# Reordering the opening of a linear-attention and MLP kernel: tile 0 alone, new load order, tile 2's x ahead of tile 3's chain

## Chip, cores, metric

The kernel runs on one core of a Trainium2 chip. The metric is the device time of one execution in microseconds (us). Most figures in the text come from profiles: a profile is the record of one execution, and its span, from the first instruction to the last, is about 2 us shorter than the time. Engines are written as in the profile: PE is TensorE, PEld its weight loads, DVE is VectorE, ACT is ScalarE, POOL is GpSimd, SP is SyncE.

## The reference

Eight batches, eight heads, 576 positions, head size 64. The attention has no softmax:

```python
kv  = einsum('bhsd,bhse->bhde', k, v)
out = einsum('bhsd,bhde->bhse', q, kv)
out = out / sqrt(mean(out*out, -1) + 1e-6) * g_norm            # per head
x   = out, heads side by side                                  # (8, 576, 512)
xn  = (x - mean(x)) / sqrt(var(x) + 1e-6) * g_ln
y   = x + relu(xn @ w1) @ w2                                   # 512 -> 2048 -> 512
```

Inputs and output are float32; the products run in bfloat16.

## The kernel before

Work is done in tiles of 128 positions; batch 0 has four (t[0] to t[3]), and 64 positions remain (`J` in the code). For each tile the chain is:

- PE turns (transposes) q, ACT copies it out of PSUM;
- PE multiplies by kv (`o`), ACT squares (`sq`), DVE sums per head (`red`), ACT takes the root (`root`), DVE inverts it (`inv`);
- DVE scales (`y`, `x`, or `x_g` in one step from a product with kv already times g), and makes the centred, bfloat16 `xc`;
- PE turns `xc`, ACT copies it out as `xT`.

Then comes the first MLP product (`mm1`): 16 groups for the four tiles of batch 0, each of 16 matmuls and followed by a relu on ACT. The second product (`mm2`) follows.

Later batches are prepared while PE is busy with the products of earlier ones. An agenda does this: `at(slot, fn)` emits `fn` just before group number `slot` of the products. Only batch 0 has no earlier products to hide behind, so its opening is written by hand:

```python
    fill(18)                       # unread matmuls on zeros, while the loads are under way
    kv_first()                     # kv of batch 0: two head pairs, copies, two more pairs, copies
    ...                            # (cut: helpers)
    half_turn(0)                   # tiles 0 and 1 together, in halves of heads
    fill(2, ps_out, "ops")
    half_o(0, 0)
    half_turn(1)
    half_o(1, 0)
    half_o(0, 1)
    half_red(0, 0)
    half_red(0, 1)
    half_o(1, 1)
    t[0].root()
    half_red(1, 0)
    half_red(1, 1)
    t[0].o_g(ps1, "p1")
    t[1].o_g(ps1, "p1")
    fill(8)
    t[0].x_g()
    t[1].root()
    halves_turn(0, halves_xc(0), ps_out, "ops")
    t[1].x_g()
    xc1 = list(halves_xc(1))
    ...                            # (cut)
    at(1, lambda: turn_first(2, ps_m, "misc", nc.vector.tensor_copy))
    at(1.1, lambda: halves_turn(1, xc1, ps_out, "ops"))
    at(1.2, o2)                    # t[2]: o, sq
    at(1.3, x2)                    # t[2]: red, y, x, xc
    at(4, lambda: turn_first(3, ps_m, "misc"))
    at(5, lambda: t[3].o())
    at(5.1, x3)                    # t[3]: sq, red, y, x, xc   (y asks for the root)
    at(6, lambda: t[2].turn(True)) # xc of tile 2: turn and copy
    at(9, lambda: turn_first(J, ps_m, "misc"))
    at(9.5, next_loads)
    at(10, lambda: t[3].turn(True))
    ...                            # (cut)
    for ts, c0, c1 in ((0, 0, 8), (1, 0, 8), (0, 8, 12), (1, 8, 12), (0, 12, 16), (1, 12, 16),
                       (2, 0, 16), (3, 0, 16)):
        mm1(0, ts, 1, c0, c1)      # tile ts, column blocks c0 to c1; a group is 4 blocks
```

The loads of batch 0 are issued in this order: k (two queues), then on one queue v in two halves, q of tiles 0 and 1 in two halves of heads, the first quarter of w1, the rest of q, the rest of w1, half of w2, batch 1, the rest of w2.

## Time and profile before

| | before |
|---|---|
| time, median of 3 runs | 291.57 us (291.55 to 291.79) |
| span of the profiled run | 289.6 us |
| PE busy | 281.9 us (97%) |
| first kv matmul | 7.56 us |
| tile 0's x turned (first transpose of `xc`) | 15.04 us |
| first product without a break from | 18.25 us |
| second product of batch 0 from | 33.37 us |
| first product of batch 1 from | 50.39 us |

The page of the kernel before, cut to three of its lines. Part 1 gives each engine's busy us, share of the span and number of instructions. In part 2 each character is a fortieth of the span (7.2 us) and gives the busy share in tenths; PEclk is the clock granted to TensorE, in tenths of full speed.

```profile
PE 281.9 (97%) x2312; PEld 158.6 (55%) x2312; DVE 151.0 (52%) x335; ACT 155.0 (54%) x339; POOL 41.0 (14%) x68
...
PEclk9999999999999999999999999999999999999999
DMA  7999999469999918995997179938202510131033
```

PE is the limit (97%), and the transfer engines are nearly full up to 50 us (0.7 in the first slice, 0.9 or more in the six after it). The timeline of the kernel before shows where PE is not full. Columns: start in us, length in us, engine, source line, operation, output<-inputs, number of instructions merged; in brackets the idle time before, and what ended it.

```profile
7.56 0.19 PE L219 MATMUL even<-v_in,k_in 64*64 64x64 bf16 x1 [0.72 <-DMA v_in<-in_v_dram]
...
15.04 0.68 PE L541 MATMUL tp<-identity,xc 128*128 128x128 bf16 x4 [0.84 <-DVE xc L532]
...
18.25 2.84 PE L402 MATMUL p<-xT_blk,w_sb 128*128 128x128 bf16 x48
...
26.63 0.75 DVE L321 SCALAR_TENSOR_TENSOR xc<-x_blk,st_blk,g_ln_sb 128x512 bf16<-128x512 f32 x1
...
27.79 0.39 PE L337 MATMUL tp<-identity,xc 128*128 128x128 bf16 x4
28.01 5.52 PE L402 MATMUL p<-xT_blk,w_sb 128*128 128x128 bf16 x96
33.37 4.48 PE L418 MATMUL p<-w_sb,m 128*128 128x512 bf16 x20
```

From 28.01 us PE does not stop: 96 matmuls in 5.52 us, then the second product. Whatever the opening saves, the rest of the kernel can only be shifted by. Tile 3's `xc` ends at 27.38 us (26.63 + 0.75), just before PE turns it at 27.79.

The chain of waits of the kernel before, from 22 to 26 us (start, length, what the end of the program is followed back to):

```profile
22.51 0.24 ACT m L405
...
23.00 0.60 ACT sq L266
...
23.62 0.70 DVE ss L287
...
24.34 0.30 ACT rms L297
24.64 0.48 ACT m L405
25.13 0.48 ACT xT_blk L339
```

This is the place that one part of the change is after. ACT squares tile 3 (23.00), then stands until DVE has summed, takes the root (24.34), then does a relu, and only then copies tile 2's `xT` (25.13), for which PE waits; the next entry of the chain is PE at 25.66.

### The profile page before, as it was taken

Reading aid. Unit: us, or ns where it says so; the run is one execution under the profiler, and the core shown is the slowest. Engines: PE = TensorE matmul, PEld = TensorE weight load, DVE = VectorE, ACT = ScalarE, POOL = GpSimd, SP = SyncE. Lnnn points to the kernel's source line nnn. Section 1 sums busy time; section 2 is a strip of 40 time slices with the busy share of each in tenths; the row PEclk is TensorE's granted clock in tenths of the full one; section 3 lists DMA queues with packets and bytes.
Section 4 is the critical chain, followed back from the end, with each engine's and each line's share of the span. In section 5 each row is a group of like instructions: output and inputs, shape, how many; then the busy total and the mean of one; then the engine's idle time right before and its main releaser. Section 6 shows DMA issues by size and latency. Waiting matters only on the chain.

```text
span 289.6 us, 5791 instructions
## 1 busy us (share of the span) xinstructions
PE 281.9 (97%) x2312; PEld 158.6 (55%) x2312; DVE 151.0 (52%) x335; ACT 155.0 (54%) x339; POOL 41.0 (14%) x68
## 2 busy tenths in 40 slices
PE   7889999999999999999999999999999999999995
PEld 2579755996569644444444444444444444444444
DVE  5775028847997793765366925762578300220022
ACT  3467755885469832882189418920894076016500
POOL 8522520032032003200410023000000000000000
PEclk9999999999999999999999999999999999999999
DMA  7999999469999918995997179938202510131033
GB/s 215 203 206 203 201 202 218 109 99 188 155 177 160 151 40 158 205 167 102 148 208 103 42 146 194 178 75 164 54 18 53 112 36 0 38 81 28 0 74 73
DMA packets 64378, 36.10 MB, mean 125 GB/s; under 512 B 31836, under 2 KB 59356, under 8 KB 64352
## 3 DMA queue, kind: packets, MB, share of 16 engines
q0 software_dynamic: 28016, 17.76, 44.2%
q1 hardware_dynamic: 35824, 17.25, 30.5%
q10 hardware_dynamic: 512, 0.72, 0.7%
q8 instruction: 18, 0.29, 0.4%
q14 instruction: 8, 0.07, 0.1%
HBM read 36.71 MB, written 9.44 MB: 159 GB/s over the span
## 4 chain that ended last, share of the span: by engine, by line
PE 93%; DMA 2%; ACT 1%; DVE 1%; POOL 1%; issue 1%; POOLq 0%
PE p L418 43%; PE p L402 43%; PE o_ps L260 3%; DMA q_in<-in_q_dram 2%; PE kv_ps L235 2%; PE tp L183 1%; PE p L196 1%; PE tp L337 1%; ACT sq L266 0%; PE tp L170 0%; PE o_half L500 0%; POOL v_in L126 0%; ACT xT_blk L542 0%; ACT m L405 0%; DVE x_blk L278 0%
## 5 line engine op out<-in xcount | busy, mean ns | idle before, releaser
L402 PE MATMUL p<-xT_blk,w_sb 128*128 128x128 bf16 (+2 forms) x1024 | 131.8, 286 | 0.2
L418 PE MATMUL p<-w_sb,m 128*128 128x512 bf16 (+2 forms) x608 | 129.2, 368 | 0.0
L405 ACT ACTIVATE m<-p 128x512 bf16<-128x512 f32 x144 | 85.5, 596 | 43.3 <-PE p L402 41.1
L402 PEld LDWEIGHTS <-w_sb 128*128 128x128 bf16 x1024 | 78.5, 98 | 44.1 <-issue 0.6
L418 PEld LDWEIGHTS <-m 128*128 128x128 bf16 x608 | 56.8, 98 | 61.8
L423 DVE SCALAR_TENSOR_TENSOR o_sb<-p,rstd,x_blk 128x512 f32<-128x512 f32 (+2 forms) x38 | 27.4, 721 | 54.3 <-PE p L418 48.7
L266 ACT ACTIVATE sq<-o_ps 128x512 f32<-128x512 f32 x34 | 20.2, 595 | 41.5 <-PE o_ps L260 41.4
L287 DVE TENSOR_REDUCE ss<-sq 128x8 f32<-128x512 f32 x34 | 23.0, 678 | 11.2 <-ACT sq L266 11.2
L329 ACT ACTIVATE dev<-x_blk,st_blk 128x512 f32<-128x512 f32 x36 | 25.7, 714 | 4.6 <-DVE st_blk L315 4.4
L321 DVE SCALAR_TENSOR_TENSOR xc<-x_blk,st_blk,g_ln_sb 128x512 bf16<-128x512 f32 x34 | 25.6, 752 | 1.2
L292 DVE TENSOR_TENSOR y<-o_ps,inv 128x512 f32<-128x512 f32 x34 | 23.5, 692 | 3.0
L311 DVE SCALAR_TENSOR_TENSOR x_blk<-y,g_norm_sb 128x512 f32<-128x512 f32 x34 | 23.5, 692 | 1.2
L411 DVE RECIPROCAL rstd<-rstd 128x4 f32<-128x4 f32 x9 | 1.6, 174 | 35.3 <-ACT rstd L410 35.3
L304 DVE RECIPROCAL inv<-rms 128x8 f32<-128x8 f32 x36 | 7.2, 201 | 23.0 <-ACT rms L297 23.0
L98 POOL COPY gate<-qt 1x1 bf16<-1x1 bf16 x5 | 0.9, 178 | 114.1 <-DMA qt<-q_p 114.1
L297 ACT ACTIVATE rms<-ss,eps_sb 128x8 f32<-128x8 f32 x36 | 10.7, 297 | 9.5 <-DVE ss L287 8.8
L260 PEld LDWEIGHTS <-qt 128*128 128x128 bf16 (+1 forms) x152 | 9.9, 100 | 7.4 <-issue 1.7
L260 PE MATMUL o_ps<-kv_pack,qt 128*128 128x128 bf16 (+1 forms) x152 | 13.3, 220 | 0.2 <-DVE qt L191 0.2
L196 PE MATMUL p<-fill_sb 128*128 128x512 bf16 x28 | 8.1, 445 | 1.2 <-DVE eps_sb L137 1.2
L329 ACT ACTIVATION_READ_ACCUMULATOR dev<-x_blk,st_blk 128x1 f32 x36 | 6.9, 190 | 0.0
L235 PEld LDWEIGHTS <-k_in 128*64 128x64 bf16 x280 | 5.0, 112 | 2.6 <-issue 2.5
L238 ACT CAST kv_pack<-kv_ps 64x256 bf16<-64x256 f32 x7 | 2.6, 366 | 7.2 <-PE kv_ps L235 7.2
(79 smaller groups left out, 116.8 us busy)
## 6 DMA issues: line engine op xcount, KB each, us to landing
out_dram<-o_sb SPq DMA_DIRECT2D x70, 128.0 KB, 2.4
w_sb<-in_moe_w_ch_dram POOLq DMA_DIRECT2D x8, 512.0 KB, 13.8
k_in<-in_k_dram POOLq DMA_DIRECT2D x7, 320.0 KB, 5.8
v_in<-in_v_dram POOLq DMA_DIRECT2D x7, 320.0 KB, 9.4
q_in<-in_q_dram POOLq DMA_DIRECT2D x7, 320.0 KB, 12.7
q_in<-in_q_dram POOLq DMA_DIRECT2D x8, 256.0 KB, 12.7
k_in<-in_k_dram POOLq DMA_DIRECT2D x7, 256.0 KB, 7.3
v_in<-in_v_dram POOLq DMA_DIRECT2D x7, 256.0 KB, 11.3
```

The costliest lines, as they stand in the source:

```text
L196: nc.tensor.matmul(p1, lhsT=fill_sb[:, :128], rhs=fill_sb, start=True, stop=True)
L260: nc.tensor.matmul(flat[rows, hp * 128:(hp + 1) * 128], lhsT=lhsT_of(hp), rhs=kvp[:, hp, :], start=True, stop=True)
L266: nc.scalar.activation(self.sq_t, self.o_ps, func=AF.Square)
L287: nc.vector.tensor_reduce(self.ss, self.sq_t, axis=AX.X, op=ALU.add)
L292: nc.vector.tensor_mul(self.y_t, self.o_ps, self.inv().to_broadcast([128, H, D]))
L311: nc.vector.scalar_tensor_tensor(x_blk[:, ts].rearrange("p (h d) -> p h d", h=H), in0=self.y_t, scalar=1.0, in1=g_norm_sb.to_broadcast([12 ...
L321: nc.vector.scalar_tensor_tensor(self.xc_t, in0=x_blk[:, self.ts], scalar=st[:, 1, self.ts:self.ts + 1], in1=g_ln_sb, op0=ALU.add, op1=ALU ...
L329: nc.scalar.activation(dev, x_blk[:, ts], func=AF.Square, bias=st[:, 1, ts:ts + 1], accum_out=st[:, 2, ts:ts + 1])
L402: nc.tensor.matmul(p1[:, i, :], lhsT=w1_sb[:, kk, de * 128:(de + 1) * 128], rhs=blk[2][:, kk, sl], start=(kk == 0), stop=(kk == nK - 1))
L405: nc.scalar.activation(m1[:, de0:de0 + per, sl], p1, func=AF.Relu)
L418: nc.tensor.matmul(p2[:, c0:c1], lhsT=m1s[b][:, de, ts * 128:(ts + 1) * 128], rhs=w2_sb[:, de, c0:c1], start=(de == 0), stop=(de == nDe - 1))
L423: nc.vector.scalar_tensor_tensor(o_sb[:, c0:c1], in0=p2[:, c0:c1], scalar=rstds[b][:, ts:ts + 1], in1=blks[b][0][:, ts, c0:c1], op0=ALU.mu ...
```

## The change

Its intent: do tile 0 alone, so that its chain is not held up by tile 1's work, with its q loaded ahead of v's last head pair; drop unread matmuls; turn and copy x of tile 2 ahead of tile 3's chain; interleave the groups of tiles 0, 1 and 2 in smaller steps; and do batch 0's second product as a half and two quarters, so that w2's last chunk is needed later. The core of the diff (cut where marked):

```diff
-    nc.gpsimd.dma_start(v_p[:, :HP // 2], pairs(v, 0, HP // 2))
-    nc.gpsimd.dma_start(v_p[:, HP // 2:], pairs(v, HP // 2, HP))
-    for h0 in (0, H // 2):
-        nc.gpsimd.dma_start(q_in[0][:64, h0:h0 + H // 2], lo(q, 0, h0, h0 + H // 2))
+    nc.gpsimd.dma_start(v_p[:, :HP - 1], pairs(v, 0, HP - 1))          # three of four pairs
+    nc.gpsimd.dma_start(q_in[0][:64, :, :2], lo(q, 0)[:, :, :2])       # q of tile 0
+    nc.gpsimd.dma_start(v_p[:, HP - 1:], pairs(v, HP - 1, HP))
+    nc.gpsimd.dma_start(q_in[0][:64, :, 2:], lo(q, 0)[:, :, 2:])
 ... (cut: kv_first becomes a class with a first part of three pairs, kv_a, and a last one, kv_b)
-    half_turn(0)
-    fill(2, ps_out, "ops")
-    ... (the order printed above)
+    kv_a.mms()
+    kv_a.copies()
+    turn_first(0, ps2, "p2")
+    kv_a.times_g()
+    kv_b.mms()
+    kv_b.copies()
+    part_o(kv_a)
+    part_o(kv_b)
+    part_sq(kv_a)
+    part_sq(kv_b)
+    kv_b.times_g()
+    part_red(kv_a)
+    part_red(kv_b)
+    turn_first(1, ps_m, "misc")
+    t[0].root()
+    t[0].o_g(ps2, "p2")
+    dead = fill(2)
+    t[1].o()
+    t[1].sq()
+    turn_first(J, ps_m, "misc")
     t[1].o_g(ps1, "p1")
-    fill(8)
+    fill(3, dead)
 ... (cut: xc of tile 0 in halves; then red, x_g, xc of tile 1)
+    def before_1():    # q of tiles 2 and 3 turned; xc of tile 1 turned; t[2]: o, sq, red, root
+    def before_2():    # t[2]: o_g, x_g, xc
+    def before_6():    # t[3]: o, sq, red, y, x, xc
-    at(4, lambda: turn_first(3, ps_m, "misc"))
-    at(5, lambda: t[3].o())
-    at(5.1, x3)
-    at(6, lambda: t[2].turn(True))
-    at(9, lambda: turn_first(J, ps_m, "misc"))
+    at(1, before_1)
+    at(2, before_2)
+    at(5, lambda: t[2].turn(True))
+    at(6, before_6)
     at(10, lambda: t[3].turn(True))
-    for ts, c0, c1 in ((0, 0, 8), (1, 0, 8), (0, 8, 12), (1, 8, 12), (0, 12, 16), (1, 12, 16),
-                       (2, 0, 16), (3, 0, 16)):
+    for ts, c0, c1 in ((0, 0, 4), (1, 0, 4), (0, 4, 8), (1, 4, 8), (0, 8, 12), (1, 8, 12),
+                       (2, 0, 12), (0, 12, 16), (1, 12, 16), (2, 12, 16), (3, 0, 16)):
         mm1(0, ts, 1, c0, c1)
-    for ts in range(4):
-        mm2_part(0, ts, p2s[ts], 0, nDe // 2)
+    for de0, de1 in ((0, nDe // 2), (nDe // 2, nDe * 3 // 4)):
+        for ts in range(4):
+            mm2_part(0, ts, p2s[ts], de0, de1)
 ... (cut: the last quarter with the evictions)
```

After, the chain starts at slot 6 and the turn stays at slot 10: four groups.

More of the change, by code (lines that the diff above doesn't have):

```diff
@@ L191, in turn_first, with fill @@
         copy(qts[0][:, i, :, :n], tp[:, :, :n])
-    def fill(n, pool=ps2, tag="p2"):
+    def fill(n, p1=None):
+        if p1 is None:
+            p1 = ps2.tile([128, 512], f32, tag="p2", name="p1")
         for _ in range(n):
-            p1 = pool.tile([128, 512], f32, tag=tag, name="p1")
             nc.tensor.matmul(p1, lhsT=fill_sb[:, :128], rhs=fill_sb, start=True, stop=True)
-            del p1
+        return p1
     def turn_q_dma(b):
@@ L205, in turn_q_dma, with __init__, mms, copies @@
         qts[b] = q_t
-    def kv_first():
-        kvp = held[0] = kv_pack[0]
-        g = g_norm_sb.to_broadcast([128, HP // 2, D])
-        for i, (pe, te, po, to) in enumerate(((ps_m, "misc", ps1, "p1"), (ps1, "p1", ps1, "p1"))):
-            even = pe.tile([128, HP // 2, D], f32, tag=te, name="even")
-            odd = po.tile([128, HP // 2, D], f32, tag=to, name="odd")
-            hps = slice(i * HP // 2, (i + 1) * HP // 2)
-            for hp in range(hps.start, hps.stop):
+    class KvFirst:
+        def __init__(self, hp0, hp1, pools):
+            self.hps, self.pools = slice(hp0, hp1), pools
+        def mms(self):
+            n = self.hps.stop - self.hps.start
+            (pe, te), (po, to) = self.pools
+            self.even = pe.tile([128, n, D], f32, tag=te, name="even")
+            self.odd = po.tile([128, n, D], f32, tag=to, name="odd")
+            for hp in range(self.hps.start, self.hps.stop):
                 for j in range(JP):
                     js = slice(j * D, (j + 1) * D)
-                    for hh, dst in ((0, even), (1, odd)):
+                    for hh, dst in ((0, self.even), (1, self.odd)):
                         rows = slice(hh * D, hh * D + D)
-                        nc.tensor.matmul(dst[rows, hp - hps.start, :], lhsT=k_p[rows, hp, js],
-                                         rhs=v_p[rows, hp, js],
+                        nc.tensor.matmul(dst[rows, hp - self.hps.start, :],
+                                         lhsT=k_p[rows, hp, js], rhs=v_p[rows, hp, js],
                                          start=(j == 0), stop=(j == JP - 1))
-            nc.vector.tensor_copy(kvp[:D, hps, :D], even[:D])
-            nc.scalar.copy(kvp[D:, hps, D:], odd[D:])
-            nc.vector.tensor_mul(kv_g[:D, hps, :D], even[:D], g[:D])
-            nc.vector.tensor_mul(kv_g[D:, hps, D:], odd[D:], g[D:])
-            del even, odd
+        def copies(self):
+            nc.vector.tensor_copy(kv_pack[0][:D, self.hps, :D], self.even[:D])
+            nc.scalar.copy(kv_pack[0][D:, self.hps, D:], self.odd[D:])
+        def times_g(self):
+            g = g_norm_sb.to_broadcast([128, self.hps.stop - self.hps.start, D])
+            nc.vector.tensor_mul(kv_g[:D, self.hps, :D], self.even[:D], g[:D])
+            nc.vector.tensor_mul(kv_g[D:, self.hps, D:], self.odd[D:], g[D:])
+            del self.even, self.odd
     def kv_of(b):
@@ L474 @@
     qts[0] = qt_pool.tile([128, JJ, HP, 128], bf16, tag="qt", name="qt")
+    held[0] = kv_pack[0]
     fill(18)
-    kv_first()
-    t = [main_tile(0, i, ps2, "p2") for i in range(4)]
-    for i in range(2):
-        t[i].ss = work.tile([128, H, 1], f32, tag="ss", bufs=4, name="ss")
-    sqs = [work.tile([128, H, D], f32, tag="sq", name="sq") for _ in range(2)]
-    banks = (((ps_out, "ops"), (ps_m, "misc")), ((ps_out, "ops"), (ps1, "p1")))
-    copies = ((nc.scalar.copy, nc.scalar.copy), (nc.vector.tensor_copy, nc.vector.tensor_copy))
@@ L486, in half_turn @@
-    def half_turn(half):
-        hp0 = half * HP // 2
-        tps = [ps2.tile([128, HP // 2, 128], bf16, tag="p2", name="tp") for _ in range(2)]
-        for i in range(2):
-            turn_groups(tps[i], i, 2 * hp0, 2 * hp0 + H // 2)
-        for i in range(2):
-            copies[half][i](qts[0][:, i, hp0:hp0 + HP // 2], tps[i])
-    def half_o(i, half):
-        hp0 = half * HP // 2
-        pool, tag = banks[half][i]
-        o = pool.tile([128, H // 2, D], f32, tag=tag, name="o_half")
-        flat = o.rearrange("p h e -> p (h e)")
-        for k2 in range(HP // 2):
-            nc.tensor.matmul(flat[:, k2 * 128:(k2 + 1) * 128], lhsT=qts[0][:, i, hp0 + k2, :],
-                             rhs=kv_pack[0][:, hp0 + k2, :], start=True, stop=True)
-        nc.scalar.activation(sqs[i][:, half * H // 2:(half + 1) * H // 2], o, func=AF.Square)
@@ L504, in half_red @@
-    def half_red(i, half):
-        hs = slice(half * H // 2, (half + 1) * H // 2)
-        nc.vector.tensor_reduce(t[i].ss[:, hs], sqs[i][:, hs], axis=AX.X, op=ALU.add)
-    half_turn(0)
-    fill(2, ps_out, "ops")
-    half_o(0, 0)
-    half_turn(1)
-    half_o(1, 0)
-    half_o(0, 1)
-    half_red(0, 0)
-    half_red(0, 1)
-    half_o(1, 1)
-    t[0].root()
-    half_red(1, 0)
-    half_red(1, 1)
-    t[0].o_g(ps1, "p1")
+    kv_a = KvFirst(0, HP - 1, ((ps_m, "misc"), (ps1, "p1")))
+    kv_b = KvFirst(HP - 1, HP, ((ps1, "p1"), (ps1, "p1")))
@@ new lines, with part_o @@
+    t = [main_tile(0, 0)] + [main_tile(0, i, *((ps1, "p1") if i == 1 else (ps2, "p2")))
+                             for i in range(1, 4)]
+    t[0].ss = work.tile([128, H, 1], f32, tag="ss", bufs=4, name="ss")
+    sq_0 = work.tile([128, H, D], f32, tag="sq", name="sq")
+    o_0 = {}
+    def part_o(kv_x):
+        hp0, hp1 = kv_x.hps.start, kv_x.hps.stop
+        o_0[hp0] = ps_out.tile([128, 2 * (hp1 - hp0), D], f32, tag="ops", name="o_part")
+        flat = o_0[hp0].rearrange("p h e -> p (h e)")
+        for hp in range(hp0, hp1):
+            nc.tensor.matmul(flat[:, (hp - hp0) * 128:(hp - hp0 + 1) * 128],
+                             lhsT=qts[0][:, 0, hp, :], rhs=kv_pack[0][:, hp, :],
+                             start=True, stop=True)
@@ new lines, in part_sq, with part_red @@
+    def part_sq(kv_x):
+        hp0, hp1 = kv_x.hps.start, kv_x.hps.stop
+        nc.scalar.activation(sq_0[:, 2 * hp0:2 * hp1], o_0.pop(hp0), func=AF.Square)
+    def part_red(kv_x):
+        hs = slice(2 * kv_x.hps.start, 2 * kv_x.hps.stop)
+        nc.vector.tensor_reduce(t[0].ss[:, hs], sq_0[:, hs], axis=AX.X, op=ALU.add)
+    kv_a.mms()
[7 more added lines that the diff above has]
+    part_sq(kv_a)
@@ L521 @@
+    part_sq(kv_b)
[3 more added lines that the diff above has]
+    turn_first(1, ps_m, "misc")
+    t[0].root()
+    t[0].o_g(ps2, "p2")
[3 more added lines that the diff above has]
+    turn_first(J, ps_m, "misc")
     t[1].o_g(ps1, "p1")
-    fill(8)
+    fill(3, dead)
+    del dead
     t[0].x_g()
-    t[1].root()
     def halves_xc(i):
@@ L534, in halves_xc, with half_turn @@
             yield xc
-    def halves_turn(i, xcs, pool, tag):
-        xT = t[i].blk[2]
-        for c, xc in enumerate(xcs):
-            tp = pool.tile([128, 2, 128], bf16, tag=tag, name="tp")
-            for kk in range(2):
-                nc.tensor.transpose(tp[:, kk, :], xc[:, kk * 128:(kk + 1) * 128], identity)
-            nc.scalar.copy(xT[:, 2 * c:2 * c + 2, i * 128:(i + 1) * 128], tp)
-    halves_turn(0, halves_xc(0), ps_out, "ops")
+    def half_turn(i, c, xc, copy):
+        tp = ps_out.tile([128, 2, 128], bf16, tag="ops", name="tp")
+        for kk in range(2):
+            nc.tensor.transpose(tp[:, kk, :], xc[:, kk * 128:(kk + 1) * 128], identity)
+        copy(t[i].blk[2][:, 2 * c:2 * c + 2, i * 128:(i + 1) * 128], tp)
+    for c, xc in enumerate(halves_xc(0)):
+        half_turn(0, c, xc, nc.scalar.copy)
+    t[1].red()
     t[1].x_g()
     xc1 = list(halves_xc(1))
-    def x2():
-        t[2].red()
-        t[2].y()
-        t[2].x()
+    def before_1():
+        turn_first(2, ps_m, "misc")
+        tp = ps2.tile([128, HP, 128], bf16, tag="p2", name="tp")
+        turn_groups(tp, 3, 0, H)
+        half_turn(1, 0, xc1[0], nc.scalar.copy)
+        t[2].o()
+        half_turn(1, 1, xc1[1], nc.vector.tensor_copy)
+        t[2].sq()
+        nc.scalar.copy(qts[0][:, 3], tp)
+        t[2].red()
+        t[2].root()
+        del tp, xc1[:]
+    def before_2():
+        t[2].o_g(ps2, "p2")
+        t[2].x_g()
         t[2].xc()
-    def x3():
+    def before_6():
+        t[3].o()
         t[3].sq()
@@ L560, in x3 @@
         t[3].xc()
-    def o2():
-        t[2].o()
-        t[2].sq()
     def next_loads():
@@ L569, in next_loads @@
         load_batch(2)
-    at(1, lambda: turn_first(2, ps_m, "misc", nc.vector.tensor_copy))
-    at(1.1, lambda: halves_turn(1, xc1, ps_out, "ops"))
-    at(1.2, o2)
-    at(1.3, x2)
-    at(4, lambda: turn_first(3, ps_m, "misc"))
-    at(5, lambda: t[3].o())
-    at(5.1, x3)
-    at(6, lambda: t[2].turn(True))
-    at(9, lambda: turn_first(J, ps_m, "misc"))
+    at(1, before_1)
+    at(2, before_2)
+    at(5, lambda: t[2].turn(True))
+    at(6, before_6)
     at(9.5, next_loads)
@@ L638 @@
         p2s[ts] = None
-        mm2_part(0, ts, p2, nDe // 2, nDe)
+        mm2_part(0, ts, p2, nDe * 3 // 4, nDe)
         finish(0, ts, p2)
```

## The prediction

> **What bounds it now.** TensorE. The busy table gives it 281.9 of 289.6 us (97%), the chain of waits 93%. From 28.0 us on its instructions are dense (the last 96 of batch 0's first product take 5.52 us), so the change can only pay in the opening. There the timeline shows: first kv matmul at 7.56 us (waits for v), first transpose of normalised x at 15.04, first product steady at 18.25, second product at 33.37. The DMA row is 99% busy at about 205 GB/s from 5 to 50 us.
>
> **What the change does, costed from the trace.**
> 1. Loads: the first kv part needs three of v's four pairs, not two. Half of v takes 1.41 us (7.56 to 8.97), so a pair costs 0.7: start near 8.27. q of tile 0 then lands near 8.9, v's last pair near 9.6. That q piece has 256-byte runs;[...] this trace has no such load to test it. I allow 0 to 1 us.
> 2. Tile 0 alone: one 0.58 us copy replaces four, two reduces (about 0.55 + 0.27) no longer queue behind tile 1's work. Followed through in-order engines, tile 0's x transposes start at 14.2 to 14.8 instead of 15.04: 0.25 to 0.9 us gained.
> 3. Tile 1 becomes later relative to tile 0: its reduce (0.69), root (0.30), reciprocal (0.20) and scaling (0.77) now follow tile 0's xc. Its xc is ready about 3.1 us after tile 0's first transposes; in before 1.9. The steady product starts near 18.3 to 19.0, after one extra turn of q (0.37): roughly even.
> 4. The copy of x of tile 2 moves ahead of tile 3's square on ScalarE. That removes a 0.3 us TensorE wait (near 25.4), but tile 3's chain starts one group later while its turn stays at slot 10. In before the chain takes 4.38 us from square (23.00) to end of xc (27.38), in time for the turn at 27.73. In after the square starts about 24.0 to 24.6, xc ends near 28.4 to 29.0, and TensorE, arriving near 27.2, **waits about 1.2 us**. Six groups follow the turn in both kernels: second product near 34.0 to 34.7.
> 5. Five fewer unread matmuls (0.216 us each): not on the chain. [...]the clock should stay full:[...] the trace shows only the warming (starts 0.425 us apart until 4.5 us, then 0.216).
> 6. Second product of batch 0 in quarters: same work, evictions bunched later; 0 to 0.3 us.
>
> **Prediction.** The early gain is given back at tile 3: net 0.5 to 1.3 us slower. **292.3 us, range 291.3 to 293.2**; faster by over 2%: 0.01; within 2%: 0.98; slower: 0.01.
>
> **Right or wrong in the profile.** First kv matmul near 8.3; x transposes of tile 0 near 14.5; a TensorE wait of about 1 us for tile 3's xc (VectorE) near 28.5; second product 0.5 to 1.3 us later than 33.37; everything after shifted by that.
>
> **What would make it wrong.** Tile 3's square starting early enough to hide the wait (then 0.3 to 0.8 us faster); three pairs of v landing before 7.8; small-run loads delaying all weights, or a cold clock; TensorE waiting for evictions at the start of batch 1.

Three passages are cut, at the marks: a remark on the 256-byte runs in point 1 and two on the clock in point 5. The sum: 0.5 to 1.3 us slower, mostly from the second product near 34.0 to 34.7 us against 33.37 (point 4). The 0 to 1 us for the 256-byte runs was an allowance of mine that no trace backed.

## More of the kernel before

The order of emission matters: in this kernel's trace ACT stands 0.75 us ahead of tile 3's root (24.34 us) while a relu and a copy that the program emits behind it become ready (PE ends their inputs at 23.59 and 23.81 us).

Note what the slots say about tile 3. Before, its chain starts at slot 5 and its turn is at slot 10: five groups of PE work, 0.89 us each (48 matmuls, three groups, take 2.68 us from 18.42 us in the chain of waits), cover the chain.

## The result

| | before | after | difference |
|---|---|---|---|
| time, median of 4 runs each | 291.63 us | 292.15 us (291.75 to 292.98) | ratio 1.0021, 95% interval 0.9996 to 1.0045 |
| time, 5 further runs of after, 9 of before | 291.69 us | 291.77 us (291.75 to 291.83) | ratio 1.0001, 0.9988 to 1.0013 |
| span of the profiled run | 289.6 us | 290.0 us | +0.4 |
| first kv matmul | 7.56 | 8.21 | +0.65 |
| tile 0's x turned | 15.04 | 14.07 | **-0.97** |
| first product without a break from | 18.25 | 18.23 (the group that starts at 17.92) | 0 |
| tile 3's `xc` turned | 27.79 | 28.17 | +0.38 |
| second product of batch 0 | 33.37 | 33.77 | **+0.40** |
| first product of batch 1 | 50.39 | 50.78 | +0.39 |

A ratio is the mean time of one kernel's fast runs over that of the other's of the same rounds, so it is not quite the ratio of the medians.

Two of the first four runs of the changed kernel (292.45 and 292.98 us) had a mean granted clock of 0.994 and 0.993; the other two (291.75 and 291.85) had 0.998 and 1.000. Three of the 27 later runs of the kernel before dipped like the first two (292.96 to 293.04 us at 0.993 and 0.994). One more, 292.92 us, was as long at 0.999, and two lay 0.4 to 0.7 us high at 0.998 (292.09 and 292.43 us); these three I cannot explain. I call the low clocks dips; more on them below. They count in the ratios. Runs without them put the changed kernel 0.1 to 0.2 us above the kernel before: the same time.

The page of the changed kernel, the line that answers to the one above:

```profile
PE 279.3 (96%) x2285; PEld 158.4 (55%) x2311; DVE 150.0 (52%) x331; ACT 155.6 (54%) x338; POOL 40.8 (14%) x68
```

PE's smaller busy time is partly bookkeeping: 2311 weight loads were recorded, but only 2285 matmuls, so 26 matmul records are missing from the trace.

The timeline of the changed kernel, same columns (lines have moved by ten: L412 is the first product, L428 the second, L331 `xc`, L347 the turn of a whole `xc`, L552 the turn in halves):

```profile
8.21 0.19 PE L224 MATMUL even<-v_in,k_in 64*64 64x64 bf16 x1 [0.96 <-DMA v_in<-in_v_dram]
...
14.07 0.68 PE L552 MATMUL tp<-identity,xc 128*128 128x128 bf16 x4 [0.54 <-DVE xc L545]
...
17.17 0.28 PE L552 MATMUL tp<-identity,xc 128*128 128x128 bf16 x2 [0.39 <-DVE xc L545]
...
17.92 1.26 PE L412 MATMUL p<-xT_blk,w_sb 128*128 128x128 bf16 x16
...
28.17 0.40 PE L347 MATMUL tp<-identity,xc 128*128 128x128 bf16 x4 [1.18 <-DVE xc L331]
28.41 5.52 PE L412 MATMUL p<-xT_blk,w_sb 128*128 128x128 bf16 x96
33.77 4.48 PE L428 MATMUL p<-w_sb,m 128*128 128x512 bf16 x19
```

The line at 28.17 us is the result in one line: PE stood 1.18 us for tile 3's `xc`. After it come the same 96 matmuls in the same 5.52 us as before.

The chain of waits of the changed kernel, from 23 us to that turn:

```profile
23.23 0.24 ACT m L415
...
23.73 0.60 ACT sq L276
...
24.35 0.70 DVE ss L297
...
25.71 0.70 DVE y L302
...
26.44 0.71 DVE x_blk L321 x2
...
27.36 0.76 DVE xc L331
```

In the kernel before, this chain left ACT after the root and went to PE through the copy of tile 2's `xT`. That copy is now early, as intended, and what decides instead is the rest of tile 3's own chain. From square to end of `xc` it takes the same as before: 23.00 to 27.38 is 4.38 us, 23.73 to 28.12 is 4.39 us.

Loads were not slower. Both profiles put GpSimd's issues from 13.49 us on down to the landing of an earlier load (it idles 1.5 to 1.9 us ahead of each), so they show the landings: before at 13.49, 16.06, 18.21, 20.76 and 23.37 us, after at 13.50, 16.06, 18.25, 20.78 and 23.41 us.

### The profile page after: what moved, and what is told of

Read it like the earlier page. It is cut to its first block, busy times and chain, and to the rows that moved or that the text cites. A ratio compares the mean times of both kernels' runs of the same rounds, so it can differ in the third digit from the quotient of the medians.

```text
span 290.0 us, 5757 instructions
## 1 busy us (share of the span) xinstructions
PE 279.3 (96%) x2285; PEld 158.4 (55%) x2311; DVE 150.0 (52%) x331; ACT 155.6 (54%) x338; POOL 40.8 (14%) x68
## 2 busy tenths in 40 slices
DMA packets 64890, 36.10 MB, mean 124 GB/s; under 512 B 32860, under 2 KB 59868, under 8 KB 64864
## 4 chain that ended last, share of the span: by engine, by line
PE 91%; DVE 3%; DMA 2%; ACT 2%; issue 1%; DVEq 0%; POOLq 0%
PE p L428 42%; PE p L412 42%; PE o_ps L270 3%; DMA v_in<-in_v_dram 2%; PE kv_ps L245 2%; PE tp L347 1%; DVE x_blk L288 0%; ACT sq L276 0%; PE tp L170 0%; DVE xc L545 0%; DVE xc L331 0%; PE odd L224 0%; ACT xT_blk L553 0%; PE tp L552 0%; DVE x_blk L321 0%
## 5 line engine op out<-in xcount | busy, mean ns | idle before, releaser
L412 PE MATMUL p<-xT_blk,w_sb 128*128 128x128 bf16 (+2 forms) x1017 | 131.3, 285 | 0.7
L428 PE MATMUL p<-w_sb,m 128*128 128x512 bf16 (+2 forms) x590 | 126.8, 368 | 1.6 <-issue 1.0
L412 PEld LDWEIGHTS <-w_sb 128*128 128x128 bf16 x1024 | 78.5, 98 | 44.2 <-issue 0.8
L428 PEld LDWEIGHTS <-m 128*128 128x128 bf16 x608 | 56.9, 98 | 61.7
L276 ACT ACTIVATE sq<-o_ps 128x512 f32<-128x512 f32 x35 | 20.8, 595 | 42.0 <-PE o_ps L270 42.0
L297 DVE TENSOR_REDUCE ss<-sq 128x8 f32<-128x512 f32 x35 | 23.7, 678 | 11.9 <-ACT sq L276 11.9
L331 DVE SCALAR_TENSOR_TENSOR xc<-x_blk,st_blk,g_ln_sb 128x512 bf16<-128x512 f32 x34 | 25.6, 752 | 1.2
L302 DVE TENSOR_TENSOR y<-o_ps,inv 128x512 f32<-128x512 f32 x33 | 22.8, 692 | 3.0
L321 DVE SCALAR_TENSOR_TENSOR x_blk<-y,g_norm_sb 128x512 f32<-128x512 f32 x33 | 22.8, 692 | 1.1
L197 PE MATMUL p<-fill_sb 128*128 128x512 bf16 x22 | 7.2, 488 | 1.2 <-DVE eps_sb L137 1.2
```

The source lines that it names most:

```text
L276: nc.scalar.activation(self.sq_t, self.o_ps, func=AF.Square)
L297: nc.vector.tensor_reduce(self.ss, self.sq_t, axis=AX.X, op=ALU.add)
L302: nc.vector.tensor_mul(self.y_t, self.o_ps, self.inv().to_broadcast([128, H, D]))
L321: nc.vector.scalar_tensor_tensor(x_blk[:, ts].rearrange("p (h d) -> p h d", h=H), in0=self.y_t, scalar=1.0, in1=g_norm_sb.to_broadcast([12 ...
L331: nc.vector.scalar_tensor_tensor(self.xc_t, in0=x_blk[:, self.ts], scalar=st[:, 1, self.ts:self.ts + 1], in1=g_ln_sb, op0=ALU.add, op1=ALU ...
L412: nc.tensor.matmul(p1[:, i, :], lhsT=w1_sb[:, kk, de * 128:(de + 1) * 128], rhs=blk[2][:, kk, sl], start=(kk == 0), stop=(kk == nK - 1))
```

## The experiments

Eleven runs were made, all with correct results (there is no e5). Theory: the early gain is given back in the wait for tile 3's `xc`, and nothing behind that wait binds. Rival: something behind it (loads, evictions, tile 1) binds, and the wait only shows it. Two further questions came up on the way: what the new loads are worth, and what the unread matmuls are for. Times are medians; "no dip" is the range of the runs with a mean granted clock of at least 0.998.

| run | edit to the changed kernel | time, us | second product at, us |
|---|---|---|---|
| e0_after_again | none | 291.77 | 33.76 |
| e1_turn3_slot11 | tile 3's turn one slot later | **290.81** | 32.87 |
| e2_turn3_slot12 | two slots later | 291.52 (1 run) | 33.54 |
| e3_square3_early_slot11 | e1, and tile 3's square a group earlier | **290.65** | 32.62 |
| e4_chain3_before_x2 | tile 3's chain ahead of tile 2's turn | 291.58 (1 run) | 33.58 |
| e6_no_fills | without the five later unread matmuls | 293.62 | 35.69 |
| e7_halves | second product in halves | 292.25, no dip 291.80 to 292.64 | 33.89 |
| e8_old_loads | loads of before | 293.84 | 36.49 |
| e9_unread_in_opening | unread matmuls: 21 first, none later | 294.03 | 36.19 |
| e10_old_loads_filled | e8 with unread matmuls in its waits | 293.25, lowest 292.94 | 35.58 |
| e11_best | e3 with four more unread matmuls | 290.71 | 32.63 |

(The second product's start is read from the timeline of the profiled run.)

### e0: the changed kernel again

> The changed kernel once more, unaltered, because two of its four runs showed a granted clock of 0.993 to 0.994 and were 0.7 to 1.2 us longer than the other two. If that dip is chance (two of nine runs of the kernel before show it as well), runs at a full clock are 291.7 to 291.9 us here too and lie 0.1 to 0.4 us above undisturbed runs of the kernel before. If the change itself provokes it, about half of the runs should dip again.

Five runs, 291.75 to 291.83 us, all at 0.998 or more. The dips of the first four runs did not come back: together the changed kernel showed two in nine runs, the kernel before three in 27. These counts are too small to say whether the change makes dips more frequent.

### e1: tile 3's turn one slot later

```diff
-    at(10, lambda: t[3].turn(True))
+    at(11, lambda: t[3].turn(True))
```

> The changed kernel with one edit: the turn of tile 3's x is asked for one slot later (11 instead of 10), so that TensorE does one more group of the first product before it needs tile 3's xc. Theory (the early gain of 0.97 us is given back in the 1.2 us wait for tile 3's xc): the wait falls from 1.2 to about 0.3 us, the second product starts near 32.9 instead of 33.8, and the time falls by about 0.9 us, to 0.4 to 0.6 us below the kernel before. Rival (the gain is lost to something behind that wait, such as loads or evictions of batch 0's second product, and the wait only shows it): the second product starts earlier but the first product of batch 1 still starts near 50.8, and the time is within 0.2 us of the changed kernel.

290.81 us, ratio to before 0.9966 (0.9950 to 0.9983). In the table of PE's waits of this run, the entry for tile 3 (total us, times, longest us):

```profile
PE tp L347 <- DVE xc L331: 0.3, 1, 0.3
```

And in its timeline:

```profile
32.87 4.48 PE L428 MATMUL p<-w_sb,m 128*128 128x512 bf16 x20
```

The wait fell from 1.2 to 0.3 us, the second product came 0.90 us earlier than in the changed kernel, the first product of batch 1 0.89 us earlier (49.89 instead of 50.78), and the time fell by 0.96 us (291.77 to 290.81). Nothing behind the wait took it back. The rival is refuted.

### e2: two slots later

```diff
-    at(10, lambda: t[3].turn(True))
+    at(12, lambda: t[3].turn(True))
```

> The changed kernel with tile 3's turn two slots later (12), directly ahead of the groups that read it. Theory: TensorE no longer waits for xc (it arrives near 28.8, xc is ready near 28.1) but then waits about 1.2 us for ScalarE's copy of the turned tile, which queues behind a relu: the wait is moved, not removed, second product near 33.8, time as the changed kernel within 0.2 us. If only the VectorE chain mattered (rival), the second product would start near 32.7.

The timeline of this run:

```profile
29.97 3.73 PE L412 MATMUL p<-xT_blk,w_sb 128*128 128x128 bf16 x64 [0.94 <-ACT xT_blk L349]
```

As expected, the wait moved to the next link: no wait for `xc`, but 0.94 us for ACT's copy of the turned tile, which has no group of products left to hide behind. My 1.2 us for it was a little high, and the single run was 0.2 us shorter than the changed kernel. A turn needs slack on both sides: far enough behind `xc`, and one group ahead of its first reader.

### e3: tile 3's square a group earlier, and slot 11

```diff
-    def before_6():
-        t[3].o(); t[3].sq(); t[3].red()
-        t[3].y() ...
+    def before_5():
+        t[3].o(); t[3].sq(); t[3].red()
+    def before_6():
+        t[3].y() ...
     at(5, lambda: t[2].turn(True))
+    at(5.5, before_5)
     at(6, before_6)
-    at(10, lambda: t[3].turn(True))
+    at(11, lambda: t[3].turn(True))
```

> As the last run, and the products, square and reduce of tile 3 are also asked for one group earlier (behind tile 2's turn, ahead of the last relu before it), while root and all that follows stay in their slot. Theory: square starts near 23.2 instead of 23.7, the wait for tile 3's xc is gone (at most 0.1 us; 0.3 us may appear as a wait for the copy of tile 3's x), second product near 32.75, time 1.1 us below the changed kernel and 0.6 to 0.8 us below the kernel before. Rival: no more than 0.2 us below the changed kernel.

The timeline of this run:

```profile
22.36 5.52 PE L412 MATMUL p<-xT_blk,w_sb 128*128 128x128 bf16 x96
27.72 0.39 PE L347 MATMUL tp<-identity,xc 128*128 128x128 bf16 x4
27.95 4.84 PE L412 MATMUL p<-xT_blk,w_sb 128*128 128x128 bf16 x80
32.62 4.48 PE L428 MATMUL p<-w_sb,m 128*128 128x512 bf16 x20
```

The square ran at 23.07 us, both waits are gone, and PE's products follow each other without a break. 290.65 us, ratio 0.9963 (0.9943 to 0.9982): 1.1 us below the changed kernel, 1.0 below the kernel before.

### e4: the order that the change undid

```diff
-    at(5, lambda: t[2].turn(True))
-    at(6, before_6)
+    at(4, before_6)
+    at(5, lambda: t[2].turn(True))
```

> The changed kernel with tile 3's whole chain asked for at slot 4, ahead of the turn and copy of tile 2's x (the order that the change undid). Theory of ScalarE as an in-order queue: the square starts near 21.8 and tile 3's xc is ready near 26, so no wait at slot 10; but ScalarE sits behind tile 3's root and copies x of tile 2 only near 24.1, so TensorE waits about 1.4 us ahead of tile 2's first group (near 23.3) instead: second product near 33.8, no gain. Rival (only tile 3's chain counts): second product near 32.6.

The timeline of this run, other engines' lines left out:

```profile
21.77 0.59 ACT L276 ACTIVATE sq<-o_ps 128x512 f32<-128x512 f32 x1
...
23.11 0.30 ACT L307 ACTIVATE rms<-ss,eps_sb 128x8 f32<-128x8 f32 x1 [0.75 <-DVE ss L297]
23.32 0.58 ACT L415 ACTIVATE m<-p 128x512 bf16<-128x512 f32 x1
...
23.80 0.57 ACT L349 COPY xT_blk<-tp 128x512 bf16<-128x512 bf16 x1
...
24.42 0.77 PE L412 MATMUL p<-xT_blk,w_sb 128*128 128x128 bf16 x11 [0.95 <-ACT xT_blk L349]
```

ACT stands 0.75 us for DVE's sum with the root at the head of its queue, while a relu and the copy that PE needs are ready behind it. So ACT keeps to the order of emission here. PE's wait of 1.2 us for tile 3 is exchanged for one of 0.95 us for tile 2, and the second product starts only 0.2 us earlier (33.58). So moving tile 2 ahead was right in itself; it only went with a chain of tile 3 that started too late for its slot.

### e7: second product in halves

```diff
-    for de0, de1 in ((0, nDe // 2), (nDe // 2, nDe * 3 // 4)):
-        for ts in range(4):
-            mm2_part(0, ts, p2s[ts], de0, de1)
+    for ts in range(4):
+        mm2_part(0, ts, p2s[ts], 0, nDe // 2)
     ...
-        mm2_part(0, ts, p2, nDe * 3 // 4, nDe)
+        mm2_part(0, ts, p2, nDe // 2, nDe)
```

> The changed kernel with the second product of batch 0 in halves again, as before the change. Theory (quarters only put off the need for w2's last chunk, which comes in time either way at this pace): no wait for the load of w2 on TensorE, first product of batch 1 near 50.8, time within 0.2 us of the changed kernel. Rival: a wait of 0.3 us or more on TensorE between 40 and 46 us for w2.

No wait for w2 in PE's waits; two runs at 291.80 and 291.86 us. These two show no gain from the quarters at this pace. Of the other two runs one dipped (293.88 us at 0.988), one took 292.64 us at a mean clock of 1.000, which I cannot explain.

### e8: the loads of before

```diff
-    (three pairs of v; q of tile 0; last pair of v; rest of q; kv in 3 + 1 pairs; q turned ahead of the last pair)
+    (v in halves; q in two halves of heads; kv in 2 + 2 pairs; q turned behind the second half)
```

> The changed kernel with the loads of before (v in halves, then q in halves of heads) and kv in 2 + 2 pairs; tile 0 is still done alone. Theory (the early gain comes from landing q of tile 0 ahead of v's last pair and whole; tile 0 alone is only possible with it): tile 0's turn waits for all heads of q (10.5 us), its x transposes start near 15.2 to 15.5 instead of 14.07, and the second product starts 1.2 to 1.4 us later than in the changed kernel, near 35.0: time about 293.0. Rival (doing tile 0 alone is what gains, the loads hardly matter): x transposes within 0.4 us of 14.07.

Tile 0's x was turned at 16.6 us, even later than expected, and the time was 293.84 us. But the profiled run is not clean: the granted clock fell to half at 11.38 us and came back at 18.21. It shows that tile 0 had to wait for the last heads of q (they let it turn at 10.64 us, as computed), not what the loads are worth. e10 was made for that. One of the four runs, though, kept its clock: 293.08 us at 0.998, 1.3 us above the changed kernel, about as expected.

### e6: without the later unread matmuls

```diff
-    dead = fill(2)
     t[1].o()
     ...
-    fill(3, dead)
-    del dead
```

> The changed kernel without its five unread matmuls behind the opening 18. Theory (they fill time in which TensorE waits, and the clock does not need them[...]): x transposes of tile 0 at 14.07 as before, matmuls of the first product still 56 ns apart, time within 0.2 us of the changed kernel. Rival (they keep the clock up): the first groups of the first product run at half rate (0.107 us a matmul) and the second product starts over 0.5 us later.

The rival was right and I was wrong. 293.62 us, 1.85 us above the changed kernel. Below are busy times by stretch, cut to PE, first of this run, then of e8, then of the changed kernel (columns: stretch in us, its length, PE busy us and instructions, granted clock, share and rate of transfers). The traces record when the granted clock changed. In both kernels, e6, e8 and e9 the changes lie whole multiples of 3.41 us apart (from one change to the next: 286.72 us, or 84 of 3.413, before; 283.31 us, or 83, after; 6.82 to 6.83 us, or two, at half clock in e6, e8 and e9), so the stretches are cut at such points: in e6 the clock rose at 3.94 us, fell at 14.18 and rose at 21.01. (The expectation of e9 below, with 1.79 us and 71%, rests on an earlier cut, which was 0.24 us too late and covered only the first five stretches of each run.)

```profile
3.94:7.36 3.42, 2.66 (x13) 1.00 1.14 295
7.36:10.77 3.41, 2.24 (x94) 1.00 1.46 193
10.77:14.18 3.41, 1.84 (x39) 1.00 1.32 203
14.18:17.60 3.42, 3.24 (x46) 0.50 1.25 206
17.60:21.01 3.41, 3.24 (x40) 0.50 1.24 207
```

```profile
7.97:11.38 3.41, 1.64 (x69) 1.00 1.29 201
11.38:14.79 3.41, 2.93 (x37) 0.50 1.33 203
```

```profile
12.10:15.51 3.41, 2.57 (x31) 1.00 1.33 202
25.75:29.16 3.41, 2.23 (x41) 1.00 1.33 202
```

In both runs a stretch with little PE work (1.84 us, 54%; 1.64 us, 48%) is followed by 6.8 us at half clock, in which the same matmuls take twice as long (16 of the first product took 2.12 us at 14.83 us in e6, and 1.06 us at 24.07). In the traces of both kernels, in every stretch at full clock that was followed by full clock and ended before PE's last work, PE was busy for at least 2.23 us (65%). And there was no long gap: PE's longest wait ahead of the drop, once it had started, was 1.6 us in e6 and 0.7 us in e8. Runs at a mean clock of 0.994, whose traces were not kept, fit one stretch at half clock (an estimate: 0.006 of 291 us, at half clock, is 3.5 us).

### e9: the unread matmuls moved into the opening

```diff
-    fill(18)
+    fill(21)
     (and none later, as in e6)
```

> The changed kernel without the five later unread matmuls, but with 21 instead of 18 in the opening. The run without the five ran 6.8 us at half clock. Theory A (what counts is TensorE's busy share in a stretch of about 3.4 us: the profile shows 1.79 us busy, 52%, in the stretch ahead of the drop, and at least 2.42 us, 71%, in all such stretches of the runs that kept their clock): matmuls in the opening do not help the stretch from 11 to 14.4 us, the clock drops again for 3.4 to 6.8 us, time 293.0 to 294. Theory B (what counts is the longest idle gap: this edit cuts the longest one, the wait for v near 8 us, from 1.6 us to 0.9 or less and leaves 1.2 us ahead of tile 0's xc, no longer than the changed kernel's gaps of 1.2 us): full clock, time 291.7 to 292.0.

294.03 us, all four runs at a mean clock of 0.986 to 0.988. In the profiled run the clock fell at 16.12 us and rose at 22.94; PE was busy for 1.88 of the 3.42 us ahead of the drop (55%):

```profile
12.70:16.12 3.42, 1.88 (x25) 1.00 1.33 204
```

Removing the longest gap did not help: PE's longest wait here was 1.2 us, while e4 kept its clock through one of 1.5 us. Theory B is refuted, and theory A fits the openings. (Theory A as I wrote it named the stretch from 11 to 14.4 us; the stretches start anew in each run, and here it was 12.70 to 16.12.)

But no single limit on this share fits the whole record. At the end of the program, where PE's work runs out, the stretch of e11 with 1.52 us of work (45%) and that of the kernel before with 1.82 us (53%) kept the clock to their ends, while e6, e8 and e9 lost it after 54%, 48% and 55%:

```profile
283.95:287.36 3.41, 1.52 (x28) 1.00 0.64 142
```

```profile
284.32:287.74 3.42, 1.82 (x33) 1.00 0.60 136
```

What is counted, and over which time, stays open; busy PE time in the profile includes modelled ends of matmuls.

### e10: the old loads at full clock

```diff
+    d0 = fill(3)
     turn_first(0, ps2, "p2")
+    fill(3, d0)
+    del d0
     (on top of e8)
```

> The run with the loads of before, with three unread matmuls ahead of tile 0's turn and three behind it, where TensorE waited for q and for the copy of q; this is to hold the clock at full, so that the loads' own cost shows. Theory: clock 1.0, tile 0's x transposes near 15.4 to 15.6 (the last heads of q land near 10.6, and the chain from there takes what it takes in the changed kernel), second product near 35.2, time 293.0 to 293.3, so the loads are worth 1.2 to 1.5 us to the changed order, more than the whole early gain of 0.97. Rival (the loss of the earlier run was the clock's): x transposes near 14.5, time below 292.3.

The clock stayed up (0.998 to 1.000 in all four runs), as theory A would have it. In the profiled run (293.55 us) the second half of v landed at 9.61 us instead of 8.97 in the kernel before, so its x transposes at 15.88 overstate the case. Two other runs took 292.94 us, 1.2 us above the changed kernel. With e8's one run at full clock (293.08 us, 1.3 us above, without the added matmuls), the new load order is worth at least about 1.2 us to the new order of work, more than the 0.97 us gained at tile 0: doing tile 0 alone needs its q whole and early. The other two runs (293.55 and 293.81 us) are longer without a dip. In the profiled one, tile 0's turn started at 11.05 us, directly behind three of the added matmuls; what they cost is not separated.

### e11: the best version, with more unread matmuls

```diff
-    fill(18)
+    fill(20)
-    fill(3, dead)
+    fill(5, dead)
     (on top of e3)
```

> Tile 3's square and reduce one group earlier and its turn at slot 11, as in the run that gave 290.65 us, with two more unread matmuls in the opening (20) and two more behind tile 1's scaled products (5 instead of 3), both in waits. Theory: same time, 290.6 to 290.7, 1.0 us below the kernel before, all runs at full clock; x transposes of tile 0 still at 14.07. Rival: the additions delay kv or tile 0's transposes by 0.1 us or more.

290.71 us, ratio to before 0.9961 (0.9944 to 0.9979), all five runs at 0.999 or more, tile 0's x at 14.09. It ties with e3. That the four extra matmuls guard against dips is plausible but not shown, since e0, e1 and e3 had none in fifteen runs either. Both beat the kernel before by 1.0 us, and by 0.3% of the time.

## Why the prediction was right, point by point

The mechanism held. The number (292.3 us) held with some luck: it is near the first median (292.15), which contains two dips; runs without dips took about 291.8 us. The wait for tile 3's `xc` was predicted at about 1.2 us near 28.5 us, and was 1.18 us up to 28.17. Both ends of it, PE's arrival and the end of `xc`, came 0.2 to 0.3 us earlier than computed, which leaves the wait as it was. e1 and e3 show that it alone stood between the changed kernel and a gain.

1. *Loads.* First kv matmul predicted near 8.27 us, measured 8.21. The allowance of 0 to 1 us for the 256-byte runs came out as zero: the page's count of packets under 512 B rose from 31836 to 32860 and later landings moved by at most 0.04 us.
2. *Tile 0 alone.* Predicted 0.25 to 0.9 us gained, measured 0.97. Slightly undersized; which term was too small is not shown.
3. *Tile 1.* Its `xc` was to be ready 3.1 us behind tile 0's first transposes: 17.17 - 14.07 = 3.10 us. The first product ran without a break from 18.23 us against 18.25 before: the gain at tile 0 was already lost here as a head start. Yet PE had less left to do: all turns of q were behind it, where the kernel before still had two (0.37 and 0.24 us in its chain of waits) and a wait of about 0.3 us for tile 2's copy. So it would have reached tile 3's turn at slot 10 near 26.83 us (an estimate: e3 turns at 27.72 without a wait, one group of 0.89 us later), 0.96 us ahead of the kernel before (27.79). That this is about tile 0's gain looks like chance, since nothing of that was left at 18.23 us. The wait took back all of it and 0.38 us more.
4. *Tile 3.* Square predicted at 24.0 to 24.6 us, measured 23.73; second product predicted 0.6 to 1.3 us later, measured 0.40. This is the mis-sized term: the square came 0.27 us ahead of the earliest time computed and the end of `xc` (28.12) 0.28 us ahead, as the first product too ran from 18.23 us instead of 18.3 to 19.0.
5. *Unread matmuls.* "Not on the chain" was right for the chain of waits and wrong as a judgement. The clock did not stay full in e6, e8 and e9: they ran 6.8 us at half clock, with no wait of PE over 1.6 us ahead of it. That the change removed five cost nothing that the undisturbed runs show; whether it made dips more frequent is open. The five that it kept are worth 1.85 us by the medians.
6. *Quarters.* 0 to 0.3 us predicted, none found (e7's two undisturbed runs).

The net: predicted 0.5 to 1.3 us slower; 0.52 by the first medians, 0.40 by the spans of the profiles, 0.1 to 0.2 by runs without dips. Part of the first figure is dips. The difference between the last two stays open: time minus span is about 2.1 us for the kernel before and about 1.75 us for the changed kernel (and 1.8 for e1, e2, e3 and e4), so some 0.35 us outside the span went the other way, and no view of the profile shows what it was.

## What to carry to other kernels

When work is moved on an engine that works in the order of emission, as ACT did here (it stood 0.75 us for one root with work ready behind it), recount the slack of what it was moved past: here tile 2's copy was freed, and tile 3's chain of 4.4 us was left with four groups (3.6 us) to hide behind where it had had five. Check both ends of a moved link, since one slot later won 0.96 us and two slots later only moved the wait to the copy. And count TensorE's busy share, stretch by stretch, before removing matmuls that nobody reads: they may be what keeps the clock (without five of them, this kernel took 1.85 us longer).
